# Expert 0 of one chunk moved to seven products, its PSUM banks taken over a chunk sooner, and the last product in two halves

## The chip, the cores and the metric

The kernel runs on one NeuronCore of one Trainium2 chip. The metric is the device time of one execution in microseconds (us). Below, TensorE is PE, VectorE is DVE, ScalarE is ACT, GpSimd is POOL and SyncE is SP; PSUM is the memory of eight banks that PE writes its results to, one bank holding 512 fp32 numbers in each of 128 partitions. A difference of about 0.2% (0.73 us) is what a measurement of this kernel can tell from no change.

## The reference, cut to what matters

Two layers follow each other. The first sorts blocks of keys and values softly (a Sinkhorn-normalised 8x8 matrix per head mixes the eight blocks), and runs attention inside each block of 96 positions. The second is a mixture of four experts over the 3072 resulting rows of 512 numbers:

```python
    p = domain_probs / (domain_probs.sum(-1, keepdims=True) + 1e-09)
    out = np.zeros((N, D), dtype=np.float32)
    for e in range(E):
        h = np.maximum(x @ w1[e], 0.0)
        out += p[:, e:e + 1] * (h @ w2[e])
```

Here N is 3072, D 512, E 4 and w1[e] is 512 x 1024. Every row goes through every expert, weighted by p.

## The kernel before, in words

**Work units.** The rows are four batches of 768; each batch is three chunks of 256 rows, so there are twelve chunks, numbered 0 to 11. Chunk g is batch `b = g // 3`, third `c = g % 3`. The attention of batches 1 to 3 is computed in small steps in the gaps ("slots") of the expert work of chunks 0 to 5; by the end of chunk 4 it is nearly done, and chunks 6 to 11 are expert work alone. The program is laid out by hand: each engine runs its instructions in the order in which the Python code issues them, and lists (`PLANS`, `PLAN_A`) say after which slot of which chunk an attention step or a sum of weight blocks is issued. An entry `(c, slot, ...)` of `PLAN_A` counts the slots of a third of batch 1: the eight groups of the first layer are slots 0 to 7, the seven products of the second layer slots 8 to 14.

**Plain first layer** (`chunk_first`): for one expert two groups of 16 matmuls of 128x256 go into a two-bank PSUM tile `ps_h`; one DVE instruction (L774) applies relu and the weight p and writes `Hb`. The tiles come from the pool `psM`, which has two places of two banks (banks 0-1 and 2-3), used in turn. Attention uses a like pool, `psA`, on banks 4 to 7.

**Seven-product first layer** (`seven`): the block of 512 x 1024 weights and the block of rows are seen as 2x2 blocks, and four output blocks come from seven products (Strassen's way, in Winograd's form) of eight matmuls of 128x128 each. This needs sums of weight blocks (`s1`, `s3`, `n2`, `s4`, made once per expert by `input_sums`, on DVE or as an ACT copy and an adding DMA issued by POOL) and sums of row blocks (`token_sums`). Its PSUM banks are single: two X, two Z, four Q. `last_banks(0)` closes `psA` and opens X, Z, Q, Q on its banks 4 to 7; `last_banks(1)` does the same for `psM` and banks 0 to 3. One matmul of 128x512 into X (L1004) is the first write of a new X bank. In each expert, p1 writes Z, ACT copies Z to X, p6 adds to X and ACT copies that to a spare SBUF tile (`last_tmp`), and so on.

**Second layer**: seven products of 16 matmuls of 128x256 for all four experts together (L753 in chunks up to 4, L1141 from chunk 5 on), summed over the experts in PSUM.

**Order around the change.** Chunk 4 (b = 1, c = 1) has a plain first layer and then its seven second-layer products on two `psM` tiles, `bankA` and `bankB` on one, `bankC` and `bankQ` on the other. In its slots the attention of batch 3 ends: `st_s` (scores), `st_a` (weights times values on PE, then `normalize` on DVE, L422 and L423), `st_x` (transposes by DMA, on SP). The last one, `st_a` of the fourth pair of heads, is in slot 14, behind the last product. Chunk 5 has expert 0 plain and experts 1 to 3 with seven products; its second layer also makes the sums of expert 0's weights on DVE (`input_sums(0, ...)`, L966). From chunk 6 on all four experts take seven products, and chunk g issues the first two products of chunk g+1's expert 0 (`last_begin`) ahead of the rest of its own last product. In chunk 11 the last product, `b22` into `bankQ`, is followed by one DVE add of 128x256 (L1197) and a store of 128 KB by SP (L1199).

Of the kernel before, what the change touches and what calls it, by code (L numbers as in the profile page):

```python
# [12 lines left out]
ALU = mybir.AluOpType  # L13
# [4 lines left out]
def kernel(  # L18
# [411 lines left out]
    def st_a(b, pr):  # L430
        if b == B - 1 and pr >= H // 2 - 2:
            xsl = Sflat[:, ds((pr + 4) * NB * 2 * D, NB * 2 * D)].rearrange("p (i h d) -> p i h d", i=NB, h=2)[0:BLK]
        else:
            xsl = att.tile([P, NB, 2, D], F16, name=f"xsl_{b}_{pr}", tag="xsl")[0:BLK]
        xsls[(b, pr)] = xsl
        vs = vss[(b, pr // 2)]
        for hh in range(2):
            ET = ETs[2 * (pr % 2) + hh]
            ps = psa([P, 2, 512], F32, f"ps_a_{b}_{pr}_{hh}")
            for i in range(NB):  # L440
                nc.tensor.matmul(  # L441
                    ps[:, i // HB, ds((i % HB) * VW, D + 1)],
                    ET[:, ds(i * BLK, P)],
                    vs[:, i, 2 * (pr % 2) + hh, 0:D + 1],
                    start=True, stop=True,
                )
            normalize(ps, xsl, hh)
# [337 lines left out]
    def chunk(b, c, slot, done=()):  # L785
# [35 lines left out]
        if b or c:  # L821
            two = [psm([P, 2, 512], F32, f"ps_p{n}_{b}_{c}") for n in range(2)]
            bankA, bankB, bankC, bankQ = [two[n // 2][:, n % 2, 0:DH] for n in range(4)]
        if b:
# [24 lines left out]
            times(bankQ, blk(1, 0), "b22", es, False)  # L849
# [99 lines left out]
    A_ORDER = (12, 13, 3, 6, 7, 8, 0, 1, 2, 9, 10, 11)  # L949
# [43 lines left out]
    last = {}  # L993

    def last_banks(n):

        (openA, openM)[n].close()
        pool = ctx.enter_context(tc.tile_pool(name=f"ps7_{n}", bufs=1, space=bass.MemoryType.PSUM, side=("right", "left")[n]))
        for nm, m in (("X", 1), ("Z", 1), ("Q", 2)):
            last[nm] = last.get(nm, []) + [  # L1000
                pool.tile([P, 512], F32, tag=f"{nm}{i}", name=f"ps_{nm}{n}{i}") for i in range(m)
            ]

        nc.tensor.matmul(last["X"][n][:], w1sb[0][:, 0, 0:P], w1sb[0][:, 1, 0:512], start=True, stop=True)  # L1004

    def last_tmp(g):
# [5 lines left out]
        for m in range(2):  # L1012
# [3 lines left out]
        for m in range(1 if g > G0 else 2):  # L1016
            t = att.tile([P, NB, 2, D], F16, name=f"tmp7x_{g}_{m}", tag="xsl").rearrange("p i h d -> p (i h d)")
            room.append(t.bitcast(F32))
# [3 lines left out]
        else:  # L1022
            last["u2"] = last["t12"] = room[0::2]
            last["u3"] = last["t22"] = room[1::2]

    def seven(g, e):

        a, t, pb = As[e], Bs[g], pbs[divmod(g, R // 2)]
        n = e - (g == G0)
        X, Z = [last[nm][n % len(last[nm])][:] for nm in ("X", "Z")]  # L1030
        u2, u3, t22, t12 = [last[nm][n % len(last[nm])] for nm in ("u2", "u3", "t22", "t12")]
        Q = last["Q"][e if n == e else (0, 0, 1, 3)[e]][:]
# [23 lines left out]
        def p1():  # L1056
            product(Z, "a11", "b11", True)
            nc.scalar.copy(X, Z)  # L1058
# [30 lines left out]
    def last_begin(g):  # L1089
        last["e0"] = seven(g, 0)  # L1090
        last["e0"][1]()
        last["e0"][5]()

    def last_chunk(g, slot=None):
        b, c = divmod(g, R // 2)
        final = g == GN - 1
        lead = int(g == G0)
        if lead:
            chunk_first(b, c, [0], 0, slot)
            last_banks(0)  # L1100
            last_tmp(g)
            prs = {1: seven(g, 1)}
            prs[1][1]()
            prs[1][5]()
            seven(g, 2)[5]()
            prs[1][2]()
            prs[1][6]()
            input_sums(0, 0, True)
            input_sums(0, 1, True)
            last_banks(1)  # L1110
        else:
            last["e0"][2]()
            prs = {0: last["e0"]}
        for e in range(1 + lead, E):
            prs[e] = seven(g, e)
        for e in range(1 + lead, E):
# [3 lines left out]
            if e > 1 + lead:  # L1120
                prs[e - 2][12]()
            if not lead or e > 2:
                now[5]()
# [12 lines left out]
        def product(ps, lhs, rhs, first=True, es=range(E), between=None, at=E - 1):  # L1136
            for e in es:
                if e == at and between:
                    between()
                for f in range(KH):  # L1140
                    nc.tensor.matmul(  # L1141
                        ps, lhs(e, f), Ts[e][rhs][:, f, :],
# [29 lines left out]
        if lead:  # L1172
            for e in range(E):
                h_sums(e, 3, True)
            input_sums(0, 2, True)
        product(bankQ, sm(0), "t1")
        nc.scalar.copy(p5[:], bankQ)
        product(bankA, sm(1), "t2", False)
        nc.scalar.copy(u2[:], bankA)
        if not lead:  # L1180
            for e in range(E):
                h_sums(e, 3, True)
        product(bankQ, blk(1, 0), "b22", False, range(2))
# [10 lines left out]
        if lead:  # L1194
            input_sums(0, 3, True)
        product(bankQ, blk(1, 0), "b22", False, range(2, E), None if final else last["e0"][6], 3)
        tt(oa2, bankQ, u2[:], ALU.add)  # L1197
        if final:
            nc.sync.dma_start(o[:, 2 * c, DH:Dm], oa2)  # L1199
        else:  # L1200
# [3 lines left out]
    PLAN_A = [  # L1204
        (1, 8, 1, 0, True), (1, 8, 1, 1, True), (1, 8, 1, 2, True), (1, 10, 1, 3, True),
# [98 lines left out]
    second_layer0(0, next_stages)  # L1304
    for qd in range(2):
        for nm in ("v", "k"):
            load_natural(1, nm, qd)
        if qd == 0:
            load_queries(1, range(2))
# [65 lines left out]
```

The softmax here doesn't subtract the row's maximum and nothing guards it: scores larger than these inputs give would overflow.

## Time and profile before

| what | value |
|---|---|
| median of 8 runs | 363.22 us (362.76 to 364.39) |
| profiled execution, its own time | 363.29 us |
| span of the profiled execution, first to last instruction | 361.5 us |
| granted PE clock | 1.00 |
| PE busy | 354.7 us (98%) |
| DVE / ACT / POOL busy | 276.8 / 173.7 / 134.2 us |
| chunk 4, second layer, first matmul | 167.39 us |
| chunk 5, first matmul | 183.46 us |
| chunk 5, second product of the second layer, first matmul | 199.05 us |
| last matmuls start / last DVE add starts / last store is issued | 357.06 / 358.20 / 358.65 us |

The profile gives, for one execution, when each instruction ran on each engine. Its time line merges equal instructions that follow each other: start, length in us, engine, line of the code, operation, tiles written and read, shapes, count; a bracket at the end gives idle time of the engine before it and who ended it. A PE instruction's length holds its passage through the array, so that rows overlap: from one row's start to the next row's start is what PE really spends. Such steps are 1.75 us for 16 matmuls of 128x256 and 0.445 us for 8 of 128x128, wherever nothing is waited for.

### The profile page before, as it was taken

The numbers are of one execution on the slowest core, as the hardware profiler recorded it, in microseconds if no ns is written. First come the engines' busy times: TensorE is split into PE (matmuls) and PEld (weight loads), VectorE is DVE, ScalarE is ACT, GpSimd is POOL, SyncE is SP. The second block draws the span as 40 slices with busy tenths as digits, with TensorE's granted clock in tenths as the row PEclk, the third lists the DMA queues.
The fourth block names the chain that finished last, engine by engine and source line by source line (L and its number), as shares of the span: only waits on it lengthen the run. The fifth ranks groups of instructions, "written<-read, shape, count | busy, mean of one in ns | idle before, by whom it ended". The sixth has DMA issues, their size and how long they took to land.

```text
span 361.5 us, 10776 instructions
## 1 busy us (share of the span) xinstructions
PE 354.7 (98%) x4589; PEld 315.6 (87%) x4589; DVE 276.8 (77%) x560; ACT 173.7 (48%) x305; POOL 134.2 (37%) x148
## 2 busy tenths in 40 slices
PE   8899999999999999999999999999999999999996
PEld 8785867888888888888889899999999998999995
DVE  5653798779788687868888978867679679687794
ACT  2664340451434355368938257175283481561740
POOL 8882110655022340000625318147065082280470
PEclk9999999999999999999999999999999999999999
DMA  7999999999999999935994210110302202103101
GB/s 101 206 206 231 208 210 203 191 196 180 188 159 144 198 128 176 162 82 71 173 204 70 60 60 2 60 60 3 97 24 45 75 3 60 61 2 66 53 15 46
DMA packets 71676, 40.47 MB, mean 112 GB/s; under 512 B 40518, under 2 KB 66380, under 8 KB 71628
## 3 DMA queue, kind: packets, MB, share of 16 engines
q0 software_dynamic: 36560, 19.93, 43.1%
q1 hardware_dynamic: 35068, 19.85, 28.4%
q8 instruction: 36, 0.59, 0.7%
q14 instruction: 12, 0.10, 0.1%
HBM read 42.00 MB, written 6.34 MB: 134 GB/s over the span
## 4 chain that ended last, share of the span: by engine, by line
PE 89%; DMA 5%; DVE 3%; ACT 1%; POOL 1%; issue 0%; DVEq 0%; ACTq 0%
PE ps_Q L1141 24%; PE ps_h L768 18%; PE ps_p L753 12%; PE ps_X L1038 10%; PE ps_Q L1038 7%; PE ps_Z L1038 7%; DMA w<-in_moe_w_dram 4%; PE ps_o L696 3%; PE ps_p L803 2%; PE ps_s L406 2%; PE ps_h L661 1%; PE ps_a L441 1%; PE ps_k L387 1%; PE ps_v L354 1%; DMA sn<-in_sort_net_dram 0%
## 5 line engine op out<-in xcount | busy, mean ns | idle before, releaser
L1051 POOL TENSOR_TENSOR Hb<-tmp,pb 128x512 f16<-128x512 f32 x40 | 50.7, 1275 | 84.8 <-ACT tmp L1050 83.5
L768 PE MATMUL ps_h<-xT,w 128*128 128x256 f16 x576 | 67.8, 273 | 0.0
L768 PEld LDWEIGHTS <-w 128*128 128x128 f16 x576 | 55.1, 98 | 7.4
L1141 PEld LDWEIGHTS <-Hb 128*128 128x128 f16 x560 | 53.4, 98 | 5.6
L774 DVE SCALAR_TENSOR_TENSOR Hb<-ps_h,pb 128x1024 f16<-128x1024 f32 x36 | 44.0, 1223 | 17.7 <-PE ps_h L768 17.5
L1038 PEld LDWEIGHTS <-w 128*128 128x128 f16 x864 | 52.4, 98 | 1.0
L1141 PE MATMUL ps_Q<-w,Hb 128*128 128x256 f16 x336 | 43.4, 273 | 0.0
L1038 PEld LDWEIGHTS <-arena 128*128 128x128 f16 x552 | 33.4, 98 | 0.3 <-issue 0.2
L413 ACT ACTIVATE ET<-ps_s 96x768 f16<-96x768 f32 x24 | 18.1, 802 | 26.5 <-PE ps_s L406 26.2
L121 POOL DMA_DIRECT2D arena<-in_q_dram x24 | 19.9, 837 | 27.9 <-DMA qT<-arena 17.8
L1038 PE MATMUL ps_X<-kT,arena 128*128 128x128 f16 x384 | 29.3, 219 | 0.1
L1074 DVE TENSOR_TENSOR tmp<-ps_Q,tmp 128x512 f32<-128x512 f32 x26 | 18.0, 692 | 14.6 <-ACT tmp L1073 10.3
L1058 ACT COPY ps_X<-ps_Z 128x512 f32<-128x512 f32 x27 | 15.4, 570 | 28.3 <-PE ps_Z L1038 27.8
L396 ACT CAST kT<-ps_k 64x384 f16<-64x384 f32 x48 | 22.7, 473 | 12.8 <-PE ps_k L387 11.8
L739 DVE TENSOR_TENSOR Sb<-Hb 128x512 f16<-128x512 f16 x45 | 26.3, 608 | 0.9 <-POOL Hb L1051 0.8
L1141 PE MATMUL ps_Q<-T,Hb 128*128 128x256 f16 x224 | 26.7, 273 | 0.0
L1050 ACT ACTIVATE tmp<-tmp 128x512 f32<-128x512 f32 x40 | 25.4, 635 | 1.2 <-DVE tmp L1074 1.0
L753 PEld LDWEIGHTS <-Hb 128*128 128x128 f16 x232 | 21.9, 98 | 3.0
L1141 PEld LDWEIGHTS <-Sb 128*128 128x128 f16 x224 | 21.9, 98 | 2.5
L1065 ACT COPY tmp<-ps_X 128x512 f32<-128x512 f32 x26 | 15.3, 587 | 13.2 <-PE ps_X L1038 13.2
L1051 POOL TENSOR_TENSOR Hb<-tmp7x,pb 128x512 f16<-128x512 f32 x14 | 19.0, 1355 | 5.7 <-ACT tmp7x L1050 5.7
L1044 DVE SCALAR_TENSOR_TENSOR Hb<-ps_X,pb 128x512 f16<-128x512 f32 x27 | 18.5, 684 | 2.7 <-PE ps_X L1038 2.7
(205 smaller groups left out, 654.3 us busy)
## 6 DMA issues: line engine op xcount, KB each, us to landing
w<-in_moe_w_dram POOLq DMA_DIRECT2D x7, 1024.0 KB, 27.6
pb<-p_dram SPq DMA_DIRECT2D x12, 512.0 KB, 5.7
arena<-in_k_dram POOLq DMA_DIRECT2D x8, 384.0 KB, 9.1
arena<-in_v_dram POOLq DMA_DIRECT2D x8, 384.0 KB, 8.4
vs<-arena SPq DMA_DIRECT2D x36, 66.0 KB, 5.5
arena<-in_q_dram POOLq DMA_DIRECT2D x24, 96.0 KB, 7.7
out_dram<-ob SPq DMA_DIRECT2D x9, 256.0 KB, 2.1
out_dram<-oa SPq DMA_DIRECT2D x8, 256.0 KB, 2.7
```

Source lines behind the costliest of these rows:

```text
L121: nc.gpsimd.dma_start(t[:, h // 2, :, h % 2, :], q[b, h].rearrange("(t p) d -> p t d", p=P))
L396: nc.scalar.copy(kT[ds(D * hh, D), r], pk[ds(D * r, D), hh].rearrange("p a (i c) -> p a i c", c=CP),)
L413: nc.scalar.activation(ETs[2 * (pr % 2) + hh][:, 0:S].rearrange("c (a x) -> c a x", a=2), pss[hh][0:BLK, :, 0:HS], AF.Exp, bias=0.0, scale ...
L739: tt(sm[0], blk(0, 1), blk(1, 1), ALU.add)
L753: nc.tensor.matmul(ps, lhs(e, f), Ts[e][rhs][:, f, :], start=(first and e == es[0] and f == 0), stop=(done and e == es[-1] and f == KH - 1 ...
L768: nc.tensor.matmul(ps[:, f, :], w1sb[e][:, kc, ds((4 * g + f) * P, P)], xT[:, kc, ds(2 * c * P, 2 * P)], start=(kc == 0), stop=(kc == NKC ...
L774: nc.vector.scalar_tensor_tensor(out=Hb[:, e, ds(4 * g, 4), :], in0=ps[:], scalar=0.0, op0=ALU.max, in1=pb[:, ds(e, 1), :].broadcast_to([P ...
L1038: nc.tensor.matmul(dst[:, ds(f * P, P)], a[lhs][:, k, ds(f * P, P)], t[rhs][:, k, :], start=(first and f == 0 and k == 0), stop=(f == KH - ...
L1044: nc.vector.scalar_tensor_tensor(out=Hb[:, e, ds(i * KH, KH), ds(j * P, P)], in0=src.rearrange("p (f x) -> p f x", f=KH), scalar=0.0, op0= ...
L1050: nc.scalar.activation(src, src, AF.Relu, bias=0.0, scale=1.0)
L1051: nc.gpsimd.tensor_tensor(Hb[:, e, ds(i * KH, KH), ds(j * P, P)], src.rearrange("p (f x) -> p f x", f=KH), pb[:, ds(e, 1), ds(j * P, P)].b ...
L1141: nc.tensor.matmul(ps, lhs(e, f), Ts[e][rhs][:, f, :], start=(first and e == 0 and f == 0), stop=(e == E - 1 and f == KH - 1), skip_group_ ...
```

## The change

Four things change together.

1. **Chunk 5, expert 0** is computed with seven products like the other three. The sums of its weight blocks are made earlier, in chunk 4's first layer: three as ACT copies with an adding POOL DMA (`PLAN_A` entries for slots 1, 2 and 4), the fourth on DVE in chunk 5's slot 0. Its third block lies in `Sb` instead of `arena`, so the last two attention outputs `xsl` move from `Sb` to `arena`, to where batch 3's values were.
2. **Banks 0 to 3 are taken over a chunk sooner**: chunk 4's second layer closes `psM` and works on the single banks X1, Z1, Q2, Q3 as `bankA`, `bankB`, `bankC`, `bankQ`. Ahead of its last product it issues p1 and p5 of chunk 5's expert 0 and the first write of X1, and inside that product p6. Chunk 5 then begins with p2 of expert 0, one slot, `last_banks(0)` and the first write of X0 (`written(0)`), another slot, and the usual order for experts 1 to 3.
3. **The last product of chunk 11** is done in two halves of 128 columns in two banks, each with its own DVE add and its own store, the first half's store issued by ACT.
4. **Two loads of batch 1's queries** go ahead of, instead of between, the loads of its values and keys on POOL.

```diff
     def st_a(b, pr):
         if b == B - 1 and pr >= H // 2 - 2:
-            xsl = Sflat[:, ds((pr + 4) * NB * 2 * D, NB * 2 * D)].rearrange("p (i h d) -> p i h d", i=NB, h=2)[0:BLK]
+            xsl = arena[:, ds((pr + 2) * NB * 2 * D, NB * 2 * D)].rearrange("p (i h d) -> p i h d", i=NB, h=2)[0:BLK]
...
-        if b or c:
+        if (b, c) == divmod(G0 - 1, R // 2):
+            last_banks(1)
+            bankA, bankB, bankC, bankQ = [last[nm][at][:, 0:DH] for nm, at in (("X", 1), ("Z", 1), ("Q", 2), ("Q", 3))]
+        elif b or c:
             two = [psm([P, 2, 512], F32, f"ps_p{n}_{b}_{c}") for n in range(2)]
...
-            times(bankQ, blk(1, 0), "b22", es, False)
+            if last["X"]:
+                last_tmp(G0, range(1), ())
+                last_begin(G0)
+                times(bankQ, blk(1, 0), "b22", es, False, True, last["e0"][6], 2)
+            else:
+                times(bankQ, blk(1, 0), "b22", es, False)
             tt(oa2, bankQ, u2[:], ALU.add)
             slot()
...
-    A_ORDER = (12, 13, 3, 6, 7, 8, 0, 1, 2, 9, 10, 11)
+    A_ORDER = (12, 13, 14, 6, 7, 8, 0, 1, 2, 9, 10, 11)
...
+    def written(n):
 
         nc.tensor.matmul(last["X"][n][:], w1sb[0][:, 0, 0:P], w1sb[0][:, 1, 0:512], start=True, stop=True)
...
-        def p1():
+        def p1(between=None):
             product(Z, "a11", "b11", True)
+            if between:
+                between()
             nc.scalar.copy(X, Z)
...
     def last_begin(g):
-        last["e0"] = seven(g, 0)
-        last["e0"][1]()
-        last["e0"][5]()
+        last["e0"] = e0 = seven(g, 0)
+        if g == G0:
+            e0[1](lambda: (e0[5](), written(1)))
+        else:
+            e0[1]()
+            e0[5]()
...
-        lead = int(g == G0)
+        lead = g == G0
+        last["e0"][2]()
         if lead:
-            chunk_first(b, c, [0], 0, slot)
+            slot()
             last_banks(0)
-            last_tmp(g)
-            prs = {1: seven(g, 1)}
-            prs[1][1]()
-            prs[1][5]()
-            seven(g, 2)[5]()
-            prs[1][2]()
-            prs[1][6]()
-            input_sums(0, 0, True)
-            input_sums(0, 1, True)
-            last_banks(1)
-        else:
-            last["e0"][2]()
-            prs = {0: last["e0"]}
...
+            written(0)
+            slot()
+            last_tmp(g, range(1, 2))
+        prs = [last["e0"]] + [seven(g, e) for e in range(1, E)]
...
-        product(bankQ, sm(0), "t1")
-        nc.scalar.copy(p5[:], bankQ)
+        ends = [(bankQ, ds(0, P), nc.scalar), (bankB, ds(P, P), nc.sync)] if final else [(bankQ, ds(0, DH), nc.sync)]
+        for bank, part, _ in ends:
+            product(bank[:, part], sm(0), "t1", part=part)
+            nc.scalar.copy(p5[:, part], bank[:, part])
...
-        product(bankQ, blk(1, 0), "b22", False, range(2, E), None if final else last["e0"][6], 3)
-        tt(oa2, bankQ, u2[:], ALU.add)
-        if final:
-            nc.sync.dma_start(o[:, 2 * c, DH:Dm], oa2)
-        else:
+        for bank, part, queue in ends:
+            product(
+                bank[:, part], blk(1, 0), "b22", False, range(early, E), None if final else last["e0"][6], 3, part
+            )
+            tt(oa2[:, part], bank[:, part], u2[:, part], ALU.add)
+            if final:
+                queue.dma_start(o[:, 2 * c, DH:Dm][:, part], oa2[:, part])
+        if not final:
             nc.sync.dma_start(o[:, 2 * c, :], oa[:])
...
     PLAN_A = [
+        (1, 1, 0, 0), (1, 2, 0, 1), (1, 4, 0, 2), (2, 0, 0, 3, True),
...
+    load_queries(1, range(2))
     for qd in range(2):
         for nm in ("v", "k"):
             load_natural(1, nm, qd)
-        if qd == 0:
-            load_queries(1, range(2))
```

## The prediction

> **What bounds the kernel now.** I read the page first, then the busy time by stages, then PE's and DVE's time lines from chunk 4's last group to chunk 5's second layer, and last the end.
>
> The page: PE is the bound, nothing else is near it.
>
> ```profile
> PE 354.7 (98%) x4589; PEld 315.6 (87%) x4589; DVE 276.8 (77%) x560; ACT 173.7 (48%) x305; POOL 134.2 (37%) x148
> ```
>
> Busy time by stages (length, then busy us and count of each engine): a chunk of seven products throughout is PE work without a hole; seven steps of 1.75 us and 28 of 0.445 make 24.70 of its 24.73. So time can be won or lost only where PE waits, and a wait of PE is lost for good: no later chunk has slack to catch up.
>
> ```profile
> 199.20:223.95 24.75, 24.75 (x339) 23.47 (x337) 20.67 (x42) 12.76 (x24) 10.32 (x9) 1.00 0.16 44
> 223.95:248.68 24.73, 24.73 (x338) 23.48 (x337) 19.45 (x40) 12.76 (x24) 10.33 (x9) 1.00 0.13 44
> ```
>
> PE's time line: second layer of chunk 4 from 167.39, its last product at 180.94, the last `st_a` at 182.69, expert 0 plain at 183.46, then experts 1 to 3. The reader is to see three places where steps are too long: 0.63 us behind 173.54 (0.44 for the same work at 178.26), 0.77 behind 182.69 (0.49 at 180.46), 0.68 behind 189.62 (0.445).
>
> ```profile
> 167.39 1.91 PE L753 MATMUL ps_p<-w,Hb 128*128 128x256 f16 x16
> ...
> 173.54 0.70 PE L406 MATMUL ps_s<-qT,kT 64*128 64x96 f16 x16
> 174.17 1.92 PE L753 MATMUL ps_p<-T,Sb 128*128 128x256 f16 x16
> ...
> 180.46 0.65 PE L441 MATMUL ps_a<-vs,ET 96*128 96x65 f16 x16
> 180.94 1.91 PE L753 MATMUL ps_p<-w,Hb 128*128 128x256 f16 x16
> 182.69 0.93 PE L441 MATMUL ps_a<-vs,ET 96*128 96x65 f16 x16
> 183.46 3.66 PE L768 MATMUL ps_h<-xT,w 128*128 128x256 f16 x32
> 186.96 0.38 PE L1004 MATMUL ps_X<-w 128*128 128x512 f16 x1
> 187.17 0.61 PE L1038 MATMUL ps_Z<-xT,w 128*128 128x128 f16 x8
> ...
> 189.62 0.61 PE L1038 MATMUL ps_Z<-xT,w 128*128 128x128 f16 x8
> 190.30 0.61 PE L1038 MATMUL ps_X<-kT,arena 128*128 128x128 f16 x8
> ```
>
> DVE's time line: who reads the banks that are handed over. The first row empties expert 3's second group of chunk 4 until 168.48, beside PE's first second-layer product, which runs on other banks; the others add chunk 4's last product (L850) and normalise the last `st_a`, until 184.47 + 0.69 = 185.16, beside expert 0's plain matmuls.
>
> ```profile
> 167.26 1.22 DVE L774 SCALAR_TENSOR_TENSOR Hb<-ps_h,pb 128x1024 f16<-128x1024 f32 x1 [0.85 <-PE ps_h L768]
> ...
> 183.07 0.41 DVE L850 TENSOR_TENSOR oa<-ps_p,u 128x256 f32<-128x256 f32 x1
> 183.41 0.19 DVE L422 RECIPROCAL rz<-ps_a 96x8 f32<-96x8 f32 x1
> ...
> 184.47 0.69 DVE L423 TENSOR_TENSOR Sb<-ps_a,rz 96x512 f16<-96x512 f32 x1
> ```
>
> **The change part by part.** All in the records of this one execution.
>
> *Expert 0's matmuls.* Out: 3.50 us (183.46 to 186.96). In: 7 x 0.445 = 3.12. **-0.38.** The two first writes of X (0.22 each) stay two.
>
> *Waits that go.* In chunk 5, 187.17 to 199.05 is 11.88 us for 21 x 0.445 + 0.22 + 1.75 = 11.31: 0.57 of waits, from expert 1 running on one X bank. In the new order experts 1 to 3 run as in chunks 6 to 11, which have none: **-0.57.** The wait inside the last `st_a` (second half waits for DVE's L423 until 183.16) goes, since three products and a first write, 3 x 0.445 + 0.22 = 1.55 us, now stand before it: 0.77 - 0.49, **-0.28.**
>
> *A wait that comes: bankA.* In the compiled program of before, expert 3's second `ps_h` tile of chunk 4 lies on banks 0 and 1, the first group's on 2 and 3, and `bankA` got the place freed first. Now `bankA` is X1, which is opened on bank 0. Its first matmul must wait for L774's 168.48, plus 0.05 as between L423's end and PE at 183.21: 168.53 instead of 167.39, **+1.14.** Behind it all of chunk 4's second layer shifts. DVE gains on PE meanwhile, and the wait at `st_s` (0.63 - 0.44) goes: **-0.19.** Bounds: 0, if X1 lay on a bank of the first group's tile (its L774 is over by 166.41); 1.56, if one DVE add of 0.42 slipped in front. I take 1.14, since row and bank are both known.
>
> *A wait that comes: X0.* In before's clock (the shift above moves PE and DVE alike): `t3` and `st_a` of the third pair end at 180.94; p1 and p5 to 181.83; first write of X1 to 182.05 (its reader L846 is over at 181.48); half of `b22` to 182.92; p6 to 183.37 (ACT's copy Z to X: two weight copies to 182.2, then 0.57 from 182.27, done 182.84, just in time); rest of `b22` to 184.24; `st_a` to 184.72; p2 to 185.17. Now `written(0)` needs bank 4, which the second half of this `st_a` fills. DVE does L850 first, which needs the end of `b22`: 0.31 to 0.48 after the last matmul's start (184.13) in L850's and L845's rows, 0.35 taken: 184.48. Then, as from 183.07 to 185.16, 2.09 us: 186.57, and PE at 186.62. Before, 3.50 us of expert 0 covered this; now p2's 0.445 does. 186.62 - 185.17 = **+1.46** (unrounded). Bounds: 0.62, if X0 needed only the first half's bank (0.84 earlier); 1.9, if DVE came 0.4 later. Waiting behind `written(0)` on PE: everything. Behind it DVE has p2's finish (0.60), the fourth sum (0.60) and `t4` (0.28): done 187.9, needed by p4 at 189.1 and p3 at 189.5: no further wait.
>
> *Sums of weights.* Three ACT copies of about 1.0 us (L968: 2.95 for three) go into chunk 4's first layer, where ACT is idle 1.40, 0.68 and 1.10 us before its rows at 156.92, 159.11 and 163.32; the second pushes the key copies by 0.3 us, to 161.4, and their reader `st_s` starts at 162.77. Cost 0; without the gaps up to 0.4 each. Their DMAs (256 KB, 6.2 us) go into POOL's idle time, 33.0 us before 171.72; they land before 172 and are read after 181. The `vs` and transposing DMAs beside them are read 10 us later. DVE loses three sums in chunk 5 and PE waited for none of them: 0.
>
> *`xsl` to `arena`.* Batch 3's values are last read at 169.14, rewritten after 181: 0.
>
> *Queries.* Two DMAs of 96 KB go past one load of values and one of keys on POOL's queue. Queries landed 0.65 us apart, so values land at 64.1 instead of 62.8 and keys at 66.1; first readers on PE: 66.39 and 69.66. SP's first transpose, which waited for them until 66.16, can go at 62.7 beside the load of `pb` that lands at 71.86 and is read at 73.26. Cost 0; if that cover is gone, up to 0.5.
>
> *The end.*
>
> ```profile
> 357.06 1.04 PE L1141 MATMUL ps_Q<-w,Hb 128*128 128x256 f16 x8
> ...
> 358.20 0.42 DVE L1197 TENSOR_TENSOR oa<-ps_Q,u 128x256 f32<-128x256 f32 x1
> ```
>
> The stores (count, KB each, median us from issue to landing); the group of two holds the last one:
>
> ```profile
> out_dram<-ob SPq DMA_DIRECT2D x9, 256.0 KB, 2.1
> out_dram<-oa SPq DMA_DIRECT2D x8, 256.0 KB, 2.7
> ...
> out_dram<-oa SPq DMA_DIRECT2D x2, 128.0 KB, 1.8
> ```
>
> 32 matmuls of 256 columns (109.2 ns) become 64 of 128 (55.7): +0.07; the last is shorter by 54 ns in its passage (273 and 219), so PE ends 0.05 later after a last step that is shorter too. The last add: 0.69 us for 512 columns, 0.42 for 256, so 0.135 less for 128. The last store goes from 128 to 64 KB: between 128 and 256 KB the rows differ by 0.3 or 0.9, with no order among the 256s, so from 0 to -0.3; 0 taken, since it ends a nearly idle queue. ACT's store starts at 358.0 and has 0.6 us in hand; before has none from ACT, so its price lies between SP's 1.8 and the 2.7 of the slowest such group: 0 to +0.3. **-0.09**, bounds -0.4 and +0.3.
>
> A rule that speaks against the halves: the Trainium skill, "DMA: Bandwidth & Descriptors", section "Anatomy of one DMA — SWDGE (gpsimd) path", fits (on POOL's path) 2.0 us fixed plus bytes over 436 GB/s. By it 128 KB takes 2.3 us, where SP's row has 1.8, so its fixed part is too high here; halving would take 0.15 off, an estimate, and the sum by the rule would be +0.94.
>
> **Sum**: -0.38 - 0.57 - 0.28 + 1.14 - 0.19 + 1.46 - 0.09 = **+1.09 us**, against the profiled 363.29 (span 361.5 and 1.8 around it): 364.38. The median is 0.07 lower, so **364.3**, +0.3%, slower by more than 0.2% (0.73 us), which is about what a measurement of this kernel tells from no change.
>
> **The rivals.**
> *bankA does not wait*: only if X1 lay elsewhere. For: before gave `bankA` the earlier place. Against: banks 0 and 4 go to X1 and X0 in before's program too. Without 1.14 - 0.19: 363.4, same.
> *X0's wait is covered*: something else stands between p2 and `written(0)`. Against: the diff has only p2 there. 362.9, same.
> *More waits follow*: expert 0 and 1 start with DVE and ACT late, as experts 1 to 3 did before (0.57), or the copy Z to X comes late (margin 0.08). For: DVE is the last to finish at three places. 364.9.
> *Faster*: banks are opened in the other order, so that each hand-over meets the bank freed first; one mechanism, deciding both waits. bankA then costs nothing (so the 0.19 stays too) and X0 0.62: -1.32 + 0.62 = -0.70, 362.5. It decides if the X0 wait is under 0.6. Against: the compiled order.
>
> **How the numbers follow.** Forecast 0.64 (its own range 363.9 to 364.8, from 0.1 per latency in each wait and the end's bounds); bankA free 0.08; X0 covered 0.07; more waits 0.14; faster 0.07. Faster by over 0.2%: 0.07; same: 0.08 + 0.07 and 0.02 of the forecast's low edge = 0.17; slower: 0.76. The range 363.1 to 365.3 leaves out the faster case and the tails.
>
> **What would show it.** In the new trace: PE's step before chunk 4's first second-layer matmul longer by 1.1 us, right at L774's end; a hole of 1.5 us before the second one-matmul row of 128x512, ended by DVE's L423; no hole in the last `st_a` nor among experts 1 to 3; a chunk period still 24.73. Wrong if X1's first write or `bankA` starts beside L774, or if expert 1's products show holes.

## The result, and the profile after

The kernel after takes 365.14 us (median of 11 runs, 364.81 to 366.76) against 363.09 us for the kernel before on the same chips (32 runs): a ratio of 1.0057, 95% interval 1.0041 to 1.0074, so slower by 0.4 to 0.7%. The profiled execution took 365.07 us (span 363.3) beside 363.29 (span 361.5): 1.78 us more. The forecast was 364.3 in a range of 363.1 to 365.3; the sign and the range held, the sum of +1.09 was about half of what came.

First the page of the kernel after, the busy time of its engines.

```profile
PE 352.6 (97%) x4645; PEld 314.6 (87%) x4645; DVE 276.3 (76%) x560; ACT 179.0 (49%) x314; POOL 139.9 (38%) x153
```

PE is busy for 2.1 us less than before (354.7), and the span is 1.8 us longer: PE stands idle for 3.9 us more. (The busy time is no measure of the matmuls saved: it counts waits that are shorter than a matmul's passage, such as the steps that were too long in the kernel before, where PE's list of waits from 160 to 200 us is empty.) The waits of PE between 160 and 200 us, by who ended them (us in total, times, longest):

```profile
PE ps_X L1012 <- DVE arena L423: 1.3, 1, 1.3
PE ps_X L753 <- DVE Hb L774: 1.0, 1, 1.0
PE ps_s L406 <- ACT arena L360: 0.5, 1, 0.5
```

The first two are the two waits of the forecast; the third comes from a step that it priced at 0. PE's time line of the same kernel, with the rows that answer to those of before:

```profile
162.84 0.21 PE L406 MATMUL ps_s<-qT,kT 64*128 64x96 f16 x1
163.54 0.50 PE L406 MATMUL ps_s<-qT,kT 64*128 64x96 f16 x15 [0.49 <-ACT arena L360]
...
167.81 0.50 PE L387 MATMUL ps_k<-arena 128*128 128x128 f16 x6
169.29 1.91 PE L753 MATMUL ps_X<-w,Hb 128*128 128x256 f16 x16 [0.98 <-DVE Hb L774]
...
175.44 0.52 PE L406 MATMUL ps_s<-qT,kT 64*128 64x96 f16 x16
175.88 1.92 PE L753 MATMUL ps_X<-T,Sb 128*128 128x256 f16 x16
...
185.96 0.65 PE L441 MATMUL ps_a<-vs,ET 96*128 96x65 f16 x16
186.44 0.61 PE L1045 MATMUL ps_Z<-xT,w 128*128 128x128 f16 x8
188.31 0.39 PE L1012 MATMUL ps_X<-w 128*128 128x512 f16 x1 [1.25 <-DVE arena L423]
188.53 0.61 PE L1045 MATMUL ps_Z<-xT,w 128*128 128x128 f16 x8
```

Steps that are too long, from start to start: 163.54 - 162.84 = 0.70 in the middle of `st_s` of slot 5, where the next score matmul elsewhere follows 0.02 later; 169.29 - 167.81 = 1.48 where 0.33 is usual behind such a row of keys (166.06 - 165.73 at the one before it), a hole of 1.14 or 1.15; 188.31 - 186.44 = 1.87 where p2 takes 0.445, a hole of 1.42. The `st_s` at 175.44 and the last `st_a` at 185.96 have lost their waits (0.44 and 0.48). DVE's time line shows who ends the two long holes.

```profile
168.01 1.23 DVE L774 SCALAR_TENSOR_TENSOR Hb<-ps_h,pb 128x1024 f16<-128x1024 f32 x1 [0.86 <-PE ps_h L768]
...
186.16 0.43 DVE L858 TENSOR_TENSOR oa<-ps_Q,u 128x256 f32<-128x256 f32 x1 [1.30 <-PE ps_Q L753]
186.50 0.19 DVE L422 RECIPROCAL rz<-ps_a 96x8 f32<-96x8 f32 x1
186.73 0.69 DVE L423 TENSOR_TENSOR arena<-ps_a,rz 96x512 f16<-96x512 f32 x1
187.34 0.19 DVE L422 RECIPROCAL rz<-ps_a 96x8 f32<-96x8 f32 x1
187.56 0.69 DVE L423 TENSOR_TENSOR arena<-ps_a,rz 96x512 f16<-96x512 f32 x1
```

168.01 + 1.23 = 169.24, PE at 169.29; 187.56 + 0.69 = 188.25, PE at 188.31. Between 186.16 and 188.25 lie the 2.09 us that the forecast took from before. From chunk 5's second layer on all is as before; the busy time by stages, over one period:

```profile
225.92:250.65 24.73, 24.73 (x338) 23.45 (x337) 19.44 (x40) 12.75 (x24) 10.31 (x9) 1.00 0.17 45
```

**Where the third wait comes from.** ACT's copy L360 and PE's scores in the kernel before, without a wait of PE:

```profile
161.42 0.80 ACT L360 CAST arena<-ps_v 128x768 f16<-128x768 f32 x1 [0.34 <-PE ps_v L354]
162.77 0.51 PE L406 MATMUL ps_s<-qT,kT 64*128 64x96 f16 x16
```

ACT's time line of the kernel after, and then the loads of `vs` that are issued at 155 to 159 us, in the kernel before and in the kernel after:

```profile
158.39 1.05 ACT L976 ACTIVATE Sb<-w 128x1024 f16<-128x1024 f16 x1
159.34 1.96 ACT L396 CAST kT<-ps_k 64x384 f16<-64x384 f32 x4
162.69 0.80 ACT L360 CAST arena<-ps_v 128x768 f16<-128x768 f32 x1 [1.39 <-DMA vs<-arena]
163.39 1.06 ACT L976 ACTIVATE Sb<-w 128x1024 f16<-128x1024 f16 x1
```

```profile
L368 SPq DMA_DIRECT2D vs<-arena x6: 577/593/598, 155.6 to 158.7; - x6
...
DMA to landing us min/median/max: 2.5/2.5/2.6
```

```profile
L368 SPq DMA_DIRECT2D vs<-arena x6: 577/593/1102, 155.6 to 158.8; - x6
...
  ACT arena L360: 1.4, 1
...
DMA to landing us min/median/max: 2.4/3.7/3.8
```

L360 copies the sorted values of the next pairs of heads into a block of `arena` that these loads still read, so it must wait for the last of them. It did so before, too: the last load landed at 161.27 there and at 162.54 now, and L360 starts 0.14 us behind that landing in all fourteen traces (the bracket of the row of before names PE's `ps_v`, which was over at 161.09). Before, each load landed 2.5 us after its issue; now they take 3.7 at the median. The second tile of scores takes the place in `psA` that `ps_v` held and that L360 empties, so from the second score matmul on PE stands behind L360. Before, L360 was over at 162.22, and with the 0.05 us that PE takes to go on this matmul, due at 162.79, had 0.52 us in hand. L360 is now 1.27 later; less those 0.52, and less the 0.07 by which PE is later itself, that gives the 0.68. What runs beside them and did not before are the adding DMAs of the weight sums on POOL (issued at 156.86 and 159.74, 256 KB each). The Trainium skill, "DMA: Bandwidth & Descriptors", section "Queues, rings and completion order", says that a DMA engine takes turns between the queues that have work for it; loads that slow down while another queue has work agree with that (2.5 to 3.7 us). Over all fourteen traces the median of these loads is 2.5 to 2.7 us in the six without the adding DMAs and 3.4 to 3.8 us in the eight with them.

**The account of the profiled difference**, by PE's rows before and after: +0.07 up to the first `st_s` of batch 1 (73.15 to 73.22; the weights that PE waits for near 29 us landed 0.77 earlier, and then PE waited 0.83 for the queries' transpose); +0.68 in slot 5; +1.15 at bankA; -0.19 at the later `st_s`; +0.26 from there to the second product of chunk 5's second layer (199.05 to 201.02); -0.20 from there to the end. Sum +1.77. When those weights land is not the change's doing: it differs between the fourteen traces, which are of one execution each, by up to 1.65 us (27.40 to 29.05). Counted from a row of batch 0's expert work near 48 us, behind that landing, the kernel after takes 2.54 us more than before (315.74 and 313.20).

### The profile page after: what moved, and what is told of

It reads as the page before. It is cut to its first block, busy times and chain, and to the rows that moved or that the text cites. A ratio compares the mean times of both kernels' runs of the same rounds, so it can differ in the third digit from the quotient of the medians.

```text
span 363.3 us, 10911 instructions
## 1 busy us (share of the span) xinstructions
PE 352.6 (97%) x4645; PEld 314.6 (87%) x4645; DVE 276.3 (76%) x560; ACT 179.0 (49%) x314; POOL 139.9 (38%) x153
## 4 chain that ended last, share of the span: by engine, by line
PE 84%; DMA 8%; DVE 3%; ACT 1%; SPq 1%; POOL 1%; issue 1%; ACTq 0%
PE ps_Q L1142 24%; PE ps_h L768 14%; PE ps_X L1045 10%; PE ps_p L753 9%; PE ps_Q L1045 7%; PE ps_Z L1045 7%; DMA w<-in_moe_w_dram 4%; DMA qT<-arena 3%; PE ps_o L696 3%; PE ps_X L753 2%; PE ps_a L441 1%; PE ps_h L661 1%; PE ps_Q L753 1%; PE ps_s L406 1%; DMA vs<-arena 1%; PE ps_v L354 1%
## 5 line engine op out<-in xcount | busy, mean ns | idle before, releaser
L1058 POOL TENSOR_TENSOR Hb<-tmp,pb 128x512 f16<-128x512 f32 x42 | 53.4, 1278 | 83.0 <-ACT tmp L1057 81.7
L768 PE MATMUL ps_h<-xT,w 128*128 128x256 f16 x544 | 64.2, 273 | 0.0
L768 PEld LDWEIGHTS <-w 128*128 128x128 f16 x544 | 52.0, 98 | 7.0
L774 DVE SCALAR_TENSOR_TENSOR Hb<-ps_h,pb 128x1024 f16<-128x1024 f32 x34 | 41.5, 1223 | 18.6 <-PE ps_h L768 18.4
L1045 PEld LDWEIGHTS <-w 128*128 128x128 f16 x896 | 54.1, 98 | 0.7
L1142 PE MATMUL ps_Q<-w,Hb 128*128 128x256 f16 (+1 forms) x352 | 43.4, 268 | 0.0
L1045 PEld LDWEIGHTS <-arena 128*128 128x128 f16 x504 | 30.2, 98 | 0.0
L1057 ACT ACTIVATE tmp<-tmp 128x512 f32<-128x512 f32 x42 | 26.6, 634 | 2.3 <-DVE tmp L1083 1.3
L739 DVE TENSOR_TENSOR Sb<-Hb 128x512 f16<-128x512 f16 x45 | 27.6, 636 | 0.0
L1045 PE MATMUL ps_X<-kT,arena 128*128 128x128 f16 x336 | 25.6, 219 | 0.0
```

Source lines behind the costliest of these rows:

```text
L739: tt(sm[0], blk(0, 1), blk(1, 1), ALU.add)
L768: nc.tensor.matmul(ps[:, f, :], w1sb[e][:, kc, ds((4 * g + f) * P, P)], xT[:, kc, ds(2 * c * P, 2 * P)], start=(kc == 0), stop=(kc == NKC ...
L774: nc.vector.scalar_tensor_tensor(out=Hb[:, e, ds(4 * g, 4), :], in0=ps[:], scalar=0.0, op0=ALU.max, in1=pb[:, ds(e, 1), :].broadcast_to([P ...
L1045: nc.tensor.matmul(dst[:, ds(f * P, P)], a[lhs][:, k, ds(f * P, P)], t[rhs][:, k, :], start=(first and f == 0 and k == 0), stop=(f == KH - ...
L1057: nc.scalar.activation(src, src, AF.Relu, bias=0.0, scale=1.0)
L1058: nc.gpsimd.tensor_tensor(Hb[:, e, ds(i * KH, KH), ds(j * P, P)], src.rearrange("p (f x) -> p f x", f=KH), pb[:, ds(e, 1), ds(j * P, P)].b ...
```

## The experiments

All are edits of the kernel after and have its arithmetic; each result is a ratio to the kernel before, run beside it on the same chip. After itself is 1.0057 [1.0041, 1.0074].

**Are the early sums what holds slot 5 up?** The three early sums by DVE, without the adding DMAs:

```diff
-        (1, 1, 0, 0), (1, 2, 0, 1), (1, 4, 0, 2), (2, 0, 0, 3, True),
+        (1, 1, 0, 0, True), (1, 2, 0, 1, True), (1, 4, 0, 2, True), (2, 0, 0, 3, True),
```

> The changed kernel with the three early weight sums of expert 0 made by single DVE instructions in the same slots of chunk 4, so that neither ACT copies nor adding DMAs stand there. Theory (the adding DMAs share the DMA engines with the `vs` stores of SP, which land 1.2 us later, ACT's L360 waits for them and so PE's `st_s` in slot 5): the hole of 0.7 us inside that `st_s` goes, the two holes at bankA and X0 stay (1.1 and 1.4 us); the time falls by 0.6 to 0.7 us, to about 364.4. Rival (the hole comes from something else, the earlier queries or the shifted lanes of POOL's queue): it stays, and the time is as that of the changed kernel within 0.2 us.

Measured 364.50, ratio 1.0044 [1.0028, 1.0060]. The hole in slot 5 is gone, the `vs` loads land in 2.6 us again, and the other two holes stay as they were. A new one of 1.02 us came before the third `st_a`: its last load of `vs` took 7.1 us and landed at 181.18. All waits above 0.2 us in PE's time line from 160 to 190 us:

```profile
167.48 1.91 PE L753 MATMUL ps_X<-w,Hb 128*128 128x256 f16 x16 [0.98 <-DVE Hb L774]
181.38 0.64 PE L441 MATMUL ps_a<-vs,ET 96*128 96x65 f16 x16 [0.86 <-ACT arena L976]
187.51 0.39 PE L1012 MATMUL ps_X<-w 128*128 128x512 f16 x1 [1.25 <-DVE arena L423]
```

(The row names ACT's copy L976, over at 181.21. But in the kernel after the same `st_a` starts at 182.17 while this copy runs until 183.02, so it doesn't wait for it; what is left is the landing.) So the sums are the cause of the hole in slot 5, but in that execution the time came back in another wait, and the ratio alone is not clear of that of after.

**ACT's copies or the DMAs?** The copies done by DVE, the adding DMAs kept:

```diff
-            nc.scalar.mul(a[dst], a[x], sign)
+            if e == 0:
+                nc.vector.tensor_scalar(out=a[dst], in0=a[x], scalar1=sign, scalar2=None, op0=ALU.mult)
+            else:
+                nc.scalar.mul(a[dst], a[x], sign)
```

> The changed kernel with the ACT copies of the three early sums made by DVE and the adding DMAs by POOL kept. Theory (the DMAs slow the `vs` stores): the hole of 0.7 us inside the `st_s` of slot 5 stays, and the `vs` stores land about 1.2 us later than in the kernel before. Rival (the three ACT copies make ACT's L360 late): the hole goes and the stores land as before.

Measured 366.71 (two runs), ratio 1.0093 [1.0061, 1.0124]. ACT has no copies there any more and stands idle, and L360 still waits for the loads; the hole in slot 5 is 1.65 us. ACT's time line, then the loads:

```profile
160.10 1.97 ACT L396 CAST kT<-ps_k 64x384 f16<-64x384 f32 x4 [0.68 <-PE ps_k L387]
164.58 0.80 ACT L360 CAST arena<-ps_v 128x768 f16<-128x768 f32 x1 [2.51 <-DMA vs<-arena]
```

```profile
DMA to landing us min/median/max: 2.4/3.4/4.2
```

So it is the adding DMAs, through the loads, and not the copies on ACT.

**Why does bankA wait?** The prediction said: X1 lies on bank 0, which expert 3's second group holds. If so, X1 on bank 2 doesn't wait:

```diff
-        for nm, at in (("X", n), ("Z", n), ("Q", 2 * n), ("Q", 2 * n + 1)):
+        for nm, at in ((("X", n), ("Z", n), ("Q", 2 * n), ("Q", 2 * n + 1)) if n == 0 else (("Q", 2), ("Q", 3), ("X", 1), ("Z", 1))):
```

> The changed kernel with the four banks taken over in chunk 4 opened in the order Q2, Q3, X1, Z1, so that bankA (X1) lies on bank 2, which expert 3's first group held, and not on bank 0. Theory: PE's step before the first product of chunk 4's second layer is 1.1 us shorter, the wait of 0.2 us at the next `st_s` comes back, the time falls by about 0.95 us, to 364.2. Rival (the pool's hand-over waits for all tiles of the old pool, whichever bank): the hole of 1.1 us stays and the time is that of the changed kernel.

Measured 364.95, ratio 1.0054 [1.0028, 1.0080]. Nothing changed: the same hole, by the same instruction.

```profile
170.14 1.91 PE L753 MATMUL ps_X<-w,Hb 128*128 128x256 f16 x16 [0.98 <-DVE Hb L774]
```

X1's first matmul, now on bank 2, starts 0.05 behind the end of the second L774 (168.86 + 1.23 = 170.09), the reader of the tile on banks 0 and 1. My reason was wrong: the bank doesn't decide. That a pool which takes the place of a closed one waits for the last reader of the whole closed pool is what the split pools below show.

**No closing of pools.** X and Z, and the two Q, become two tiles of two banks from the old pools:

```diff
-        (openA, openM)[n].close()
...
-            last[nm][at] = pool.tile([P, 512], F32, tag=f"{nm}{at}", name=f"ps_{nm}{at}")
+        two = [(psa, psm)[n]([P, 2, 512], F32, f"ps_{nm}{n}") for nm in ("XZ", "QQ")]
...
+            last[nm][at] = two[m // 2][:, m % 2, :]
```

> The changed kernel without closing the two PSUM pools: the X and Z, and the two Q, are taken as one more two-bank tile each from the old pools, so that X1 and Z1 get the place of expert 3's first group, X0 and Z0 that of the first half of the last `st_a`. Opening the banks in another order did not move either hole. Theory now (closing a pool makes every bank of the new one wait for the last reader of the whole old one): the hole of 1.1 us at bankA goes and the one at X0 shrinks from 1.4 to about 0.6 us; the wait of 0.2 us in the next `st_s` comes back; 1.8 us in all, to about 363.3. Rival (it is the one L774, and the last normalisation, whatever the tile): both holes keep their length, 365.1.

Measured 445.74, ratio 1.2272 [1.2242, 1.2302]. The hand-over did what was expected, bankA without a wait and X0 with 0.58, and everything behind it was ruined: X and Z now are one tile, and a matmul into X waits for the reader of Z. PE's waits over the whole execution, and the rows of the hand-overs:

```profile
PE ps_XZ L1044 <- DVE Hb L1050: 25.3, 38, 1.2
PE ps_QQ L1044 <- DVE tmp L1082: 19.2, 13, 1.6
```

```profile
167.84 0.50 PE L387 MATMUL ps_k<-arena 128*128 128x128 f16 x6
168.18 1.91 PE L753 MATMUL ps_XZ<-w,Hb 128*128 128x256 f16 x16
...
187.14 0.39 PE L1011 MATMUL ps_XZ<-w 128*128 128x512 f16 x1 [0.42 <-DVE arena L423]
```

The same with DVE's sums and with the last `st_a` issued sooner (the edit is told below) met the same fate.

```diff
+                times(bankQ, blk(1, 0), "b22", es, False, True, lambda: (last["e0"][6](), slot()), 2)
...
+        two = [(psa, psm)[n]([P, 2, 512], F32, f"ps_{nm}{n}") for nm in ("XZ", "QQ")]
...
+        (1, 1, 0, 0, True), (1, 2, 0, 1, True), (1, 4, 0, 2, True), (2, 0, 0, 3, True),
```

> The same without closing the pools, with the three early sums on DVE and the last `st_a` inside the last product. Theory: none of the three holes is left, and what stays of the prediction are its gains (0.38, 0.57, 0.28 and 0.1 us): 1.3 us under the kernel before, about 361.6. Rival (the next thing late takes their place, as in the run with the sums on DVE, where the third `st_a` waited 1.0 us for the last `vs` store, which landed at 181.2 as in the changed kernel but was needed sooner): a hole of up to 1.5 us before that `st_a`, and the time is that of the kernel before, 362.9.

Measured 444.39, ratio 1.2239 [1.2198, 1.2280]; its trace has none of the three holes, but a wait of 0.43 us for the shared tile of X and Z ahead of the last product, and chunks 5 to 11 are ruined as before.

**Two pools of one place each.** This keeps X and Z apart, and closes the places one by one, the place that is free first for X and Z:

```diff
-    psM = openM.enter_context(tc.tile_pool(name="psM", bufs=2, space=bass.MemoryType.PSUM))
+    psMs = [openM.enter_context(tc.tile_pool(name=f"psM{n}", bufs=1, space=bass.MemoryType.PSUM)) for n in range(2)]
...
+        pairs = ((("X", n), ("Z", n)), (("Q", 2 * n), ("Q", 2 * n + 1)))
+        for part in (pairs, pairs[::-1])[n]:
```

(`psA` likewise; tiles are taken from the two in turn.)

> The kernel after, with the two places of each PSUM pool made two pools of one place each, so that a hand-over closes them one by one: X1 and Z1 lie on the banks of expert 3's first group, free at about 166.4, and X0 and Z0 on the banks of the first half of the last st_a. All work is the same. My theory, that closing a pool makes its successor wait for the last reader of the whole pool: the hole of 1.14 us at bankA goes and the wait of 0.19 at the scores comes back; the hole of 1.42 at X0 shrinks to about 0.58 (the second half's normalisation, 0.84, is no longer waited for); the hole of 0.66 in the scores of slot 5 stays. Sum -1.14 + 0.19 - 0.84 = -1.8: 363.3 by the median of after. The rival, that DVE's lateness moves the wait elsewhere: the same work of DVE is waited for in the next rows (the products that read its Hb, or p6 and p2), and the time stays above 364.5.

Measured 363.62, ratio 1.0010 [0.9996, 1.0024]: no longer to be told from before, and 0.47% of it won back, 1.7 us, where 1.8 was expected. PE's time line:

```profile
167.02 0.50 PE L390 MATMUL ps_k<-arena 128*128 128x128 f16 x6
167.36 1.91 PE L756 MATMUL ps_X<-w,Hb 128*128 128x256 f16 x16
...
173.51 0.70 PE L409 MATMUL ps_s<-qT,kT 64*128 64x96 f16 x16
174.14 1.92 PE L756 MATMUL ps_X<-T,Sb 128*128 128x256 f16 x16
...
185.84 0.39 PE L1019 MATMUL ps_X<-w 128*128 128x512 f16 x1 [0.42 <-DVE arena L426]
```

bankA starts 0.34 after the key row, without a wait; the 0.63 at the next `st_s` (0.19 of wait) is back; X0's hole is 0.58 instead of 1.42. This settles that both waits of the hand-over come from closing whole pools, and that DVE's lateness does not turn up elsewhere.

**Cover for X0.** The last `st_a` issued sooner, inside the last product behind p6:

```diff
-                times(bankQ, blk(1, 0), "b22", es, False, True, last["e0"][6], 2)
+                times(bankQ, blk(1, 0), "b22", es, False, True, lambda: (last["e0"][6](), slot()), 2)
```

(and no slot behind the product.)

> The changed kernel with the last `st_a` (slot 14 of chunk 4) issued inside the last product, right behind p6, instead of behind the product and its DVE add. Theory (X0's wait is the normalisation of this `st_a`, which DVE can only start behind L850): the normalisation starts about 1 us sooner, the hole before X0's first write shrinks from 1.4 to about 0.4 us, the time falls by about 1.0 us, to 364.1. Rival (the hole is set by something else on DVE or by the room of the pool): the hole keeps its length and the time stays.

Measured 363.99, ratio 1.0029 [1.0009, 1.0050]. X0's hole fell from 1.42 to 0.46, since half a product more stands between the last `st_a` and `written(0)`; the holes in slot 5 and at bankA stayed. So X0's wait is a matter of what stands between.

**Three of these together**: DVE's sums and the early last `st_a`, by the edits shown above, and X and Z opened behind the Qs in both places:

```diff
-        for nm, at in (("X", n), ("Z", n), ("Q", 2 * n), ("Q", 2 * n + 1)):
+        for nm, at in (("Q", 2 * n), ("Q", 2 * n + 1), ("X", n), ("Z", n)):
```

> The changed kernel with the sums on DVE, with the last `st_a` inside the last product, and with both sets of four banks opened with the two Q first, so that X0 lies on bank 6 and X1 on bank 2. Theory: all three holes go (0.7, 1.1 and 1.4 us; the wait of 0.2 us in `st_s` comes back); the changed kernel's 365.1 falls by about 3.0 us to 362.1, which is 1.0 under the kernel before: what the prediction's gains without its two waits come to. Rival (PE only changes the place where it waits, DVE being the next to be late): the holes come back in experts 0 and 1 of chunk 5, and the time is not below that of the kernel before, 363.1.

Measured 363.22, ratio 1.0016 [0.9999, 1.0033]. Slot 5 has no hole, X0's is 0.46, bankA's 1.14 stays once more. The wait before the third `st_a`, which DVE's sums alone had brought, did not come. Another, of 0.49 us, came at 124 us, ahead of all that was edited:

```profile
123.98 0.66 PE L441 MATMUL ps_a<-vs,ET 96*128 96x65 f16 x16 [0.32 <-DMA vs<-arena]
168.40 1.91 PE L753 MATMUL ps_X<-w,Hb 128*128 128x256 f16 x16 [0.98 <-DVE Hb L774]
```

**The queries' order**, put back as before:

```diff
-    load_queries(1, range(2))
     for qd in range(2):
         for nm in ("v", "k"):
             load_natural(1, nm, qd)
+        if qd == 0:
+            load_queries(1, range(2))
```

> The changed kernel with the loads of batch 1's queries back between those of its values and keys. Theory (the first `st_s` waits for a transpose that lands at about 73 us in either order, since it queues behind the load of `pb` and shares the DMA engines with the same bytes): the time is that of the changed kernel within 0.3 us. Rival (the earlier queries made that transpose land later, and the 0.9 us that PE stood there are a loss): 0.5 to 0.9 us less, and the transpose lands before 72.5.

Measured 364.97, ratio 1.0053 [1.0034, 1.0072], the same as after. In its trace PE does not wait for the queries, and loses 0.62 us at 124.40 instead. What the order does to the queries' transpose (`qT`, issued by SP at 62.1 in the kernel after, at 65.9 with the order put back) is seen in the time to landing, first after, then with the old order:

```profile
  PE ps_s L406: 0.8, 1
DMA to landing us min/median/max: 11.0/11.0/11.0
```

```profile
DMA to landing us min/median/max: 6.7/6.7/6.7
```

Issued 3.8 us sooner it lands no sooner (73.1 and 72.6): in all fourteen traces, of both orders, it lands 0.2 to 0.9 us behind the second load of keys, which goes on POOL's queue beside it. Between the two kernels this is not to be seen in the time; the last experiment comes back to it.

**The halves**, undone: the last product whole, one store of 128 KB.

```diff
-        ends = [(bankQ, ds(0, P), nc.scalar), (bankB, ds(P, P), nc.sync)] if final else [(bankQ, ds(0, DH), nc.sync)]
+        ends = [(bankQ, ds(0, DH), nc.sync)]
```

> The kernel after, with its last product whole again: one bank, one DVE add of 256 columns, one store of 128 KB by SP. The prediction gave the halves -0.09 (bounds -0.4 and +0.3), so this would take 0.1 longer than after: 365.2. From after's trace (last store landed 1.65 us after its issue, before's 1.83) I now expect 0.1 to 0.2 longer. The rival, that ACT's store of the first half costs something: 0.1 to 0.3 shorter than after. The last matmuls, the add and the store should lie as in before, moved by a constant.

Measured 364.61, ratio 1.0057 [1.0038, 1.0075]: equal to after, the halves are too small to be timed. In the traces, from chunk 11's load of `pb` to the end of the span: after 327.83 to 363.29, 35.46 us; whole 326.96 to 362.61, 35.65, and before 325.88 to 361.52, 35.64. So the halves are worth 0.19 us. The last store of 64 KB landed 1.65 us after its issue, that of 128 KB 1.82. ACT's store of the first half landed at 362.14, SP's of the second at 362.32: ACT's doesn't end the kernel.

**All three holes.** Split pools, DVE's sums and the early last `st_a`:

```diff
-                times(bankQ, blk(1, 0), "b22", es, False, True, last["e0"][6], 2)
+                times(bankQ, blk(1, 0), "b22", es, False, True, lambda: (last["e0"][6](), slot()), 2)
...
-        (1, 1, 0, 0), (1, 2, 0, 1), (1, 4, 0, 2), (2, 0, 0, 3, True),
+        (1, 1, 0, 0, True), (1, 2, 0, 1, True), (1, 4, 0, 2, True), (2, 0, 0, 3, True),
```

(and the split pools of above.)

> The kernel with split pools, and with the three early weight sums made wholly by DVE, and with the last st_a issued inside the last product behind p6. If the three holes are the whole loss: bankA 0, X0 0.2 or less, scores in slot 5 0: about 364.9 - 0.95 - 1.3 - 0.66 = 362.0, some 1.0 us under before. The rival, which the kernel with DVE's sums alone speaks for: the loads of vs for the third pair land too late for its st_a as soon as PE is earlier there, and 0.9 to 1.5 us of what is won is waited away again: 363.0 to 363.5, the same as before.

Measured 362.62, ratio 0.9989 [0.9972, 1.0006], runs from 361.43 to 363.94. In its trace (an execution of 363.94) none of the three holes is left, nor the one before the third `st_a`; the only wait of over 0.2 us between 70 and 200 us is again the one near 125 us, 0.89 us long.

```profile
125.79 0.66 PE L444 MATMUL ps_a<-vs,ET 96*128 96x65 f16 x16 [0.73 <-DMA vs<-arena]
```

**The same with the queries' old order** (the edit shown above, and nothing else):

```diff
-    load_queries(1, range(2))
...
+        if qd == 0:
+            load_queries(1, range(2))
```

> The kernel with split pools, DVE's early sums and the early last st_a, and with the queries' loads back between the loads of values and keys, as before. Counted from a row of batch 0's expert work near 48 us to the end of the span, the kernel of the last run but without queries took 312.9 with a hole of 0.9 at 125 us that lies ahead of every changed place, so 312.0 without it, where before took 313.2. My theory: the queries' order costs nothing that repeats, so the time is the same as with the new order, 362.3 to 362.9, some 0.5 under before, and the stretch is 312.0 plus whatever the loads of vs at 125 us cost in this execution. The rival: the new order makes PE wait at the first scores of batch 1, up to 1 us in some executions; then the old order gives 361.9 or less, at least 1.0 under before.

Measured 361.60 (12 runs, 361.47 to 362.47), ratio 0.9961 [0.9947, 0.9974]: faster than before by 0.3 to 0.5%, 1.45 us, and 3.5 us under the kernel after. The time is the rival's: the old order is worth about 1 us beside the kernel with the new one (ratios 0.9989 and 0.9961; the two intervals together leave 0.2 to 1.8 us). Its mechanism is not shown here: in the one trace of the kernel with the new order PE does not wait at the first scores, and the fastest runs of both are equal (361.43 and 361.47), so what the order costs it costs in some executions. PE works without a wait through both hand-overs; the busy time by stages:

```profile
160.00:200.00 40.00, 40.00 (x558) 36.33 (x556) 34.60 (x68) 30.85 (x51) 18.77 (x16) 1.00 0.77 126
```

From a row of batch 0's expert work near 48 us to the end of the span this execution takes 312.12 us, before 313.20, after 315.74.

## Why the prediction was right in sign and half as large as the result

**Right, by their own terms.** bankA: +1.14 forecast, 1.14 measured, ended by L774. X0: +1.46 forecast, 1.42 measured, by the very chain of L850's successor (L858) and two normalisations. The waits that go, at `st_s` (-0.19) and in the last `st_a` (-0.28), and experts 1 to 3 without holes (-0.57) went as said. From bankA's start to the second product of chunk 5's second layer the terms give -0.38 - 0.57 - 0.28 + 1.46 - 0.19 = +0.04; the rows give +1.97 - 1.90 = +0.07. This part of the working held to a few hundredths of a microsecond.

**Right in length, wrong in reason: bankA.** "I take 1.14, since row and bank are both known": the row was, the bank didn't matter. X1 on bank 2 waited as long, and so the lower bound of the step ("0, if X1 lay on a bank of the first group's tile") was no bound. The same holds of X0: with the whole pool closed it needed both halves of the last `st_a`, whichever bank it lay on (with the early last `st_a` the hole is 0.46 with X0 on bank 4 and on bank 6); with the pool split 0.58 was left, near the lower bound of 0.62. The rival "banks are opened in the other order" could therefore not have happened by an order alone.

**The term that failed: "Sums of weights. ... Cost 0".** It cost 0.68 us in the profile. ACT's three copies fitted in its gaps as said, and the hole stayed without them. The failing sentence is the one on the DMAs beside them: "The `vs` and transposing DMAs beside them are read 10 us later." I asked when the data of the loads is needed, and not who waits to overwrite what they read: L360 rewrites the block of `arena` that they read, in slot 5. Before, that copy already ran right behind the last landing (161.42 and 161.27), with only the 0.52 us behind it as cover for PE, and both were in the trace. With +0.68 in this place the sum would have been +1.77, the difference of the profiles; that it fits to the hundredth is luck, since what else was off cancels (+0.07 up to the first scores, +0.01 at bankA, +0.03 from there to chunk 5's second layer, -0.11 at the end).

**The end**: -0.09 forecast, -0.19 by the traces; the last store's 0 (bounds 0 to -0.3) should have been about -0.17 (1.82 to 1.65). ACT's store cost nothing.

**Queries: "Cost 0; if that cover is gone, up to 0.5."** The step looked only at when the queries can be issued. In the traces with the new order PE waited for them at the first scores 0.83 (after), 1.07, 1.78 and 0.31 us in four, 0.22 or less in the others; with the old order in none of three. In after's own profile the wait of 0.83 was made up by a start that was 0.77 earlier, so it doesn't show in the 1.77. In the medians, +2.05, some 0.3 stays beyond the profiles' 1.77; a wait that comes in some executions would fit: over the eleven traces with the new order it is 0.4 us in the mean, an estimate from one execution of each kernel. The two comparisons are too coarse to settle it: put back alone, the old order won 0.1 us, give or take 0.9 (the two 95% intervals together); put back in the kernel without holes it won 1.0, give or take 0.8. So the cost of this step, taken as 0, is some tenths of a microsecond as far as is known, and how it comes about stays open.

**Chances.** The rival "more waits follow" (364.9) is nearest in time, but by another mechanism than it named: neither expert 0 or 1 nor the copy Z to X was late. The measured 365.14 lies above the forecast's own range (363.9 to 364.8) and inside the stated one (up to 365.3) because that had room for this rival; that the missed wait was of about its size is luck.

## What to carry to other kernels

Ask of every DMA beside an added transfer not only who reads what it brings, but who waits to overwrite what it reads: 1.2 us of slower loads became 0.7 us of idle PE through a copy that nobody had on the list. Hand over PSUM place by place: a pool that is closed as a whole makes its successor wait for its last reader, and the remedy is several pools of one place, not another order of banks and not one larger tile. A change that is slower by the sum of three waits may hold a faster one: with the waits taken away one by one, and its move of the queries' loads undone, the change gave 0.4% less time than before.

## What the runs showed of the hardware

- Six loads of 66 KB on SP's queue landed in 2.5 us each with POOL's queue idle (2.5 to 2.6), and in 2.4 to 4.2 us beside adding DMAs of 256 KB on POOL's queue; in the busier stretch at 170 us the last of six took 5.5 to 7.1 us from one kernel to the next.
- A transposing DMA issued 3.8 us sooner landed no sooner: 11.0 instead of 6.7 us, each time close behind a load of keys on another queue.
- Of the loads of `vs` near 115 us, which no edit touched, the last took 4.7 to 6.9 us (6.0 before) in the eleven traces in which PE doesn't wait for it, and 7.3, 7.3 and 7.7 us in the three in which PE stood 0.49, 0.62 and 0.89 us at 124 to 126 us. Such waits come with both orders of the queries and with three different kernels; what decides them was not tried.
- A store of 64 KB at the end landed in 1.65 us, one of 128 KB in 1.82. The fit that the prediction weighed (the Trainium skill, "DMA: Bandwidth & Descriptors", section "Anatomy of one DMA — SWDGE (gpsimd) path") is for POOL's path; its 0.15 for the difference, an estimate, agrees with SP's 0.17 here, and its fixed 2.0 us is above both of SP's times.
